# Softmax statistics of the plain attention heads: grouped scaling of maxima, a sum step for each tile, another order of the first head's tiles

## The chip, the cores and the metric

One core of a Trainium2 chip runs the whole program. The metric is device time in microseconds (us), the median of three runs. The engines named below are TensorE (PE, its weight loads PEld), VectorE (DVE), ScalarE (ACT), GpSimd (POOL) and SyncE (SP, which issues most DMAs).

## The reference, cut to what matters

Three stages follow one another. The first is attention over 4 batches of 8 heads, 576 rows of 64 columns each, with a mask in blocks of 64 rows. Only this stage is touched:

```python
scores = scale * np.matmul(q, k.transpose(0, 1, 3, 2))
scores = np.where(mask, scores, -1000000000.0)
scores = scores - np.max(scores, axis=-1, keepdims=True)
attn = np.exp(scores)
attn = attn / (np.sum(attn, axis=-1, keepdims=True) + 1e-09)
return np.matmul(attn, v)
```

The second stage is `h = max(x@w1, x@w2, x@w3)` and `h @ w_out` over all 2304 rows (512 to 768 to 512). The third sends each row to its two best of 8 experts (512 to 1024 to 512) and adds the weighted results.

## The kernel before, in words

**Attention.** A head has 576 rows, which is four and a half tiles of 128 rows. Tiles 0 and 1 see at most 256 keys; tiles 2, 3 and 4 see up to 384, 512 and 576 keys. The heads of the first batch (`i < NF`, NF = 8) are "plain": their scores are one float32 matmul. From the second batch on, heads use a split into two float32r parts and, for tiles 2 and 3, a fused VectorE instruction for the maximum.

- `s2(i)` (tile 4, 576 keys, in the two-bank PSUM tile `a2`), `s1(i)` (tile 2, 384 keys, one bank `s`) and `s3(i)` (tile 3, 512 keys, one bank `s`) make the scores and probabilities of the three large tiles of head i. Each calls `exps`: a maximum by VectorE (L240), its scaling by 0.125 (L241), and the exponential by ScalarE (L242), which also gives the sum of the row. Probabilities go to `Pa` and `Pb`, two of each.
- The three sums of a head lie in one statistics tile `st`. Only `s3` closes them: `inverse` adds 1e-9 (L245) and takes the reciprocal (L246) of three columns at once, and `scale_by` multiplies the three tiles (L253 on VectorE; L251 on ScalarE for tile 3 of the first three heads, `NRM[1]`).
- Tiles 0 and 1 are done two heads at a time: a "pair" gives four parts (128, 256, 128 and 256 keys) in `first_scores` (scores L444), which calls `soft`. The four pairs of the first batch come first in the program; their sums are not applied to the probabilities but spread by transposes (L522) in `first_rest`. The four pairs of the second batch are done beside plain heads 1 to 4, with scaling on VectorE. Pairs 1 and 3 of the first batch use the two banks of `a2`, the others two banks `s`.
- `t1` and `t2` transpose the probabilities (L304), `pv` multiplies them by the values (L357 for plain heads).

**Beside it.** `widen` converts the weights of the second stage: for each piece VectorE does L575 and L576, ScalarE L577 and L587, GpSimd L582, L585 and mostly L588. `hidden` (L662 to L664) is the second stage's first matmul; it needs a group of converted weights and finished rows of attention, and fills TensorE between the steps of the heads.

**What sets the order.** The loop over heads runs the steps of the string `ORDER = 's2 s1 g fr g t1 s3 t2 g fv fs g p g v pf g'`; s2, s1 and s3 there are those of head i+1, `g` is a piece of weight conversion and of the second stage, `fs` and `fr` are the pairs. Ahead of the loop, head 0 gets s2, s1, s3 by hand. This program order is only a priority: a planner goes through it with planned durations, and on every engine puts forward later work when earlier work is not ready by its plan. The order in which it leaves the instructions is then fixed for each engine, and each engine carries them out strictly in that order. Statistics tiles `st` have three buffers, so a fourth must wait until the first is released.

Of the kernel before, what the change touches and what calls it, by code (L numbers as in the profile page):

```python
# [13 lines left out]
AF = mybir.ActivationFunctionType  # L14
OP = mybir.AluOpType
AX = mybir.AxisListType
# [20 lines left out]
NF = 8  # L37
# [4 lines left out]
NRM = (0, 3, 0, 0)  # L42
# [7 lines left out]
NP, NK, NQ = 2, 2, 2  # L50
# [5 lines left out]
def plain(ap):  # L56
    return ap.bitcast(F32)
# [3 lines left out]
def tile_attention_moe_moe(ctx, tc, qT, kT, v, w1, w2, w3, w_out, gates, noise, e1, e2, out):  # L61
    nc = tc.nc
# [80 lines left out]
    PA = [att.tile([128, 384], F32, name=f"Pa{j}") for j in range(NP)]  # L143
    PB = [att.tile([128, 1088], F32, name=f"Pb{j}") for j in range(NP)]
# [44 lines left out]
    def prep_head(i):  # L189
        if i < NF:  # L190
            QK[i] = RAW.pop(i)
            return
        q, k = RAW.pop(i)
        Qs = att.tile([128, 384], F32R, name="Qs", bufs=NQ)
        Kh = att.tile([128, S], F32R, name="Kh", bufs=NK)
        Kl = att.tile([128, S], F32R, name="Kl", bufs=NK)
        nc.scalar.activation(Qs, q, AF.Copy)
        nc.scalar.activation(Kh, k, AF.Copy)
        nc.gpsimd.tensor_sub(Qs[64:], q[64:], plain(Qs[64:]))
        nc.gpsimd.tensor_sub(Kl, k, plain(Kh))  # L200
        QK[i] = (Qs, Kh, Kl)
# [9 lines left out]
    def masked(ps, o):  # L211

        nc.tensor.matmul(ps[:, o:o + 64], mL, mask[:, 448:], start=False, stop=True)

    def scores(ps, i, t, k0, k1, diag=None):
        if i < NF:
            q, k = QK[i]
            nc.tensor.matmul(ps, q[:D, 128 * t - 256:128 * t - 128], k[:D, k0:k1], start=True, stop=diag is None)
            if diag is not None:
                masked(ps, diag)  # L220
            return
        Qs, Kh, Kl = QK[i]
        lt = Qs[:, 128 * t - 256:128 * t - 128]
        nc.tensor.matmul(ps, lt, Kh[:, k0:k1], start=True, stop=False)
        nc.tensor.matmul(ps, lt, Kl[:, k0:k1], start=False, stop=True)

    def stats():
        return att.tile([128, 4, 4], F32, name="st", bufs=3)

    def exps(st, j, src, dst, fused):  # L230
        scale = 0.125
        if fused:

            w = src.shape[-1]
            nc.vector.tensor_tensor_reduce(out=dst, in0=src, in1=mask[:, 512 - w:], scale=-scale, scalar=3.0e38,
                                           op0=OP.add, op1=OP.min, accum_out=st[:, 1, j:j + 1])
            src, scale = dst, -1.0
        else:
            ax = AX.XY if len(src.shape) == 3 else AX.X
            nc.vector.tensor_reduce(st[:, 0, j:j + 1], src, axis=ax, op=OP.max, negate=True)  # L240
            nc.vector.tensor_scalar(st[:, 1, j:j + 1], st[:, 0, j:j + 1], scale, None, op0=OP.mult)  # L241
        nc.scalar.activation(dst, src, AF.Exp, bias=st[:, 1, j:j + 1], scale=scale, accum_out=st[:, 2, j:j + 1])  # L242

    def inverse(st, n):
        nc.vector.tensor_scalar(st[:, 2, :n], st[:, 2, :n], 1.0e-9, None, op0=OP.add)  # L245
        nc.vector.reciprocal(st[:, 3, :n], st[:, 2, :n])  # L246
        return st[:, 3]

    def scale_by(st, j, dst, norm=False):
        if norm:  # L250
            nc.scalar.activation(dst, dst, AF.Copy, scale=st[:, 3, j:j + 1])  # L251
        else:
            nc.vector.tensor_scalar(dst, dst, st[:, 3, j:j + 1], None, op0=OP.mult)  # L253

    def soft(parts, scaled=True, fused=False):
        st = stats()
        for j, (src, dst) in enumerate(parts):
            exps(st, j, src, dst, fused)
        inv = inverse(st, len(parts))
        if not scaled:  # L260

            return inv
        for j, (src, dst) in enumerate(parts):
            scale_by(st, j, dst)

    def bank(kind="m"):
        n, c = TAGS[kind]
        return (psS if n == "s" else psT).tile([128, 512], F32, name=n, bufs=c)


    ST = {}

    def s1(i):
        ps = bank("s")[:, :384]
        scores(ps, i, 2, 0, 384, 320)
        exps(ST[i], 1, ps, PA[i % NP], i >= NF)

    def s3(i):
        Pa, Pb, st = PA[i % NP], PB[i % NP], ST.pop(i)
        ps = bank("s")  # L280
        scores(ps, i, 3, 0, 512, 448)
        exps(st, 2, ps, Pb[:, 576:], i >= NF)

        inverse(st, 3)
        scale_by(st, 0, Pb[:, :576])
        scale_by(st, 1, Pa)
        scale_by(st, 2, Pb[:, 576:], i < NRM[1])

    def s2(i):
        Pb = PB[i % NP]  # L290
        ST[i] = stats()
        ps = psS.tile([128, 2, 512], F32, name="a2")
        scores(ps[:, 0, 0:288], i, 4, 0, 288)
        scores(ps[:, 1, 0:288], i, 4, 288, 576)
        exps(ST[i], 0, ps[:, :, 0:288], Pb[:, :576].rearrange("p (a b) -> p a b", a=2), False)

    POFF = {2: (PA, 0), 3: (PB, 576), 4: (PB, 0)}

# [133 lines left out]
    def first_scores(data, P, two=False, scaled=True):  # L432
        q, k = data[:2]
        parts = []
        if two:
            pair = psS.tile([128, 2, 512], F32, name="a2")
        for r in range(2):
            m = slice(64 * r, 64 * r + 64)
            ps = pair[:, r] if two else bank("s")
            for t in range(2):  # L440
                o = 128 * t
                n = o + 128
                a, b = (q, k[:, r]) if len(k.shape) == 3 else (q[m], k[m])
                nc.tensor.matmul(ps[:, o:o + n], a[:, o:o + 128], b[:, :n], start=True, stop=False)  # L444
                masked(ps, o + n - 64)
                parts.append((ps[:, o:o + n], P[:, 384 * r + o:384 * r + o + n]))
        return soft(parts, scaled)


    FR, FQ, FT = {}, {}, []  # L450
# [33 lines left out]
    def f_scores(b, h):  # L484
        Qs, Kh, Kl, _ = FQ[b, h]
        ps = bank("s")
        for t in range(2):
            p, lt = ps[:, 256 * t:256 * t + 256], Qs[:, 128 * t:128 * t + 128]
            nc.tensor.matmul(p, lt, Kh, start=True, stop=False)
            nc.tensor.matmul(p, lt, Kl, start=False, stop=True)  # L490
        soft([(ps[:, 0:128], FP[:, 0:128]), (ps[:, 256:512], FP[:, 128:384])], fused=True)
# [374 lines left out]
    def weights(n):  # L866
        for _ in range(n):
            next(conversion, None)

    weights(1)  # L870
    warm(bank(), WM[0])
    inv = first_scores(FIRST[0], PB[0], A2 & 1, False)
    for j in range(4):
        weights(WS[0])
        if j < 3:
            nxt = first_scores(FIRST[j + 1], PB[(j + 1) % NP], A2 >> (j + 1) & 1, False)
        first_rest(FIRST[j], PB[j % NP], PB[j % NP], 0, j, inv)
        inv = nxt
        weights(WS[1])
# [3 lines left out]
    load_head(1)  # L883
    load_values(1)
    weights(WS[4])
    s2(0)
    s1(0)
    s3(0)
    prep_head(1)
    weights(WS[2])  # L890
    cost = [0.0]
# [21 lines left out]
    for i in range(NH):  # L913
        b, h = divmod(i, H)
# [16 lines left out]
        for o in ORDER.split():  # L931
# [11 lines left out]
            elif o == "pf":  # L943
                if i + 1 in FI:
                    prep_f(*FI[i + 1])
                if i + 2 in FI:
                    load_f(*FI[i + 2])
            elif o == "fs":
                if i in AI:
                    first_scores(later.pop(), FP)  # L950
                    if order:
                        later.append(load_later(*order.pop(0)))
                if i in FI:
                    f_scores(*FI[i])
            elif o == "fr":
                if i - 1 in AI:
                    fb, j = AI[i - 1]
                    first_rest(now.pop(), FP, FP, 2 * fb, j)
                    if j == 3:
                        ready.add(2 * fb)  # L960
                if i in AI:
                    now.append([load_later_v(*AI[i])])
                if i - 1 in FI:
                    f_turn(*FI[i - 1])
            elif o == "fv":
                if i - 1 in FI:
                    f_values(*FI[i - 1])
            elif o[0] == "t":
                (t1, t2)[int(o[1]) - 1](i)
            elif i + 1 < NH:  # L970
                {"s1": s1, "s2": s2, "s3": s3}[o](i + 1)
# [16 lines left out]
    def bank2():  # L988
        turn[0] ^= 1
        if turn[0]:  # L990
            return ps2.tile([128, 512], F32, name="b")
        return psT.tile([128, 512], F32, name="t", bufs=4)
# [150 lines left out]
    ps = bank2()  # L1143
# [77 lines left out]
    with tc.If(full > 0):  # L1221
# [10 lines left out]
        with tc.For_i(0, E) as e:  # L1232
# [4 lines left out]
            with tc.For_i(0, NT) as t:  # L1237
# [6 lines left out]
                ps = ps3.tile([128, 4, 128], F32, name="pa")  # L1244
# [66 lines left out]
```

## Time and profile before

| | us |
|---|---|
| median of 3 runs | 1087.37 |
| lowest and highest | 1085.68, 1087.65 |
| the profiled execution | 1087.95 |
| its span | 1086.1 |
| PE busy in the span | 1034.8 |
| DVE, ACT, POOL busy | 537.9, 459.1, 533.3 |

The profiled execution's time has 1.85 us around its span. The plain heads and the pairs lie in the first 215 us; after that come the heads of the other batches (up to 543 us) and the experts.

### The profile page before, as it was taken

The page shows a single profiled execution, that of the slowest core. Times are in us where ns is not written, and L with a number is a line of the kernel's source. Part 1 is how long each engine was busy: PE and PEld are TensorE (multiplying, and loading weights), DVE is VectorE, ACT ScalarE, POOL GpSimd, SP SyncE. Part 2 cuts the span into 40 slices and gives each one's busy share as a digit, 9 for nine tenths or more (in the row PEclk, how much of TensorE's full clock was granted, in tenths as well). Part 3 has the DMA queues.
Part 4 walks back from the last instruction along what each step waited for, and adds up shares of the span by engine and source line. Part 5 has one row for each costly group of instructions (what it writes and reads, how often), then busy time and mean ns, then how long its engine had stood idle before and what let it go on. Part 6 is the DMA issues. An engine that isn't in the chain of part 4 may idle for free. (4 is left out here: it accounts for less than half of the span.)

```text
span 1086.1 us, 18720 instructions
## 1 busy us (share of the span) xinstructions
PE 1034.8 (95%) x6721; PEld 917.4 (84%) x6721; DVE 537.9 (50%) x1552; ACT 459.1 (42%) x1138; POOL 533.3 (49%) x465
## 2 busy tenths in 40 slices
PE   8799999999979999799999999989999999999997
PEld 4466678998879989799999997979898898989895
DVE  7789746596796887756333632222132222222221
ACT  5656555565765666554311433323232322323110
POOL 4447503455556464451321448877474646656302
PEclk7698999998989999899999999999999999999999
DMA  9533312152442323211020236655443444443101
GB/s 232 160 93 125 106 47 63 34 157 58 144 150 65 113 63 100 70 26 39 24 80 21 69 118 206 198 167 169 130 159 121 143 146 146 137 136 114 57 20 63
DMA packets 78513, 115.93 MB, mean 107 GB/s; under 512 B 17976, under 2 KB 48184, under 8 KB 78416
## 3 DMA queue, kind: packets, MB, share of 16 engines
q1 hardware_dynamic: 67824, 85.28, 26.3%
q0 software_dynamic: 10592, 29.41, 8.3%
q8 instruction: 54, 0.88, 0.3%
q14 instruction: 43, 0.35, 0.1%
HBM read 95.18 MB, written 20.53 MB: 107 GB/s over the span
## 5 line engine op out<-in xcount | busy, mean ns | idle before, releaser
L132 POOL TENSOR_TENSOR w<-rw,w 128x1536 fp32r<-128x1536 f32 (+1 forms) x45 | 141.1, 3142 | 74.2 <-ACT w L131 63.9
L131 ACT ACTIVATE w<-rw 128x1536 fp32r<-128x1536 f32 (+1 forms) x45 | 60.2, 1343 | 114.4 <-DMA rw<-in_e 65.0
L662 PE MATMUL t<-xA,w 128*128 128x256 f32 x360 | 105.2, 294 | 1.5 <-ACT w L587 0.8
L664 PE MATMUL t<-xA,w 128*128 128x256 f32 x360 | 103.9, 289 | 0.0
L663 PE MATMUL t<-xA,w 128*128 128x256 f32 x360 | 103.7, 289 | 0.1
L1041 PE MATMUL b<-xh,w 128*128 128x384 f32 (+7 forms) x272 | 86.8, 320 | 0.9 <-ACT xh L1031 0.9
L1042 PE MATMUL b<-xl,w 128*128 128x384 f32 (+7 forms) x272 | 86.9, 320 | 0.2 <-DVE xl L1032 0.2
L1043 PE MATMUL b<-xh,w 128*128 128x384 f32 (+7 forms) x272 | 86.9, 319 | 0.0
L662 PE MATMUL t<-xB,w 128*128 128x256 f32 x288 | 83.7, 291 | 1.4 <-DVE st L241 1.2
L677 POOL TENSOR_TENSOR hl<-hm,hh 128x512 fp32r<-128x512 f32 x24 | 31.6, 1318 | 105.2 <-ACT hh L676 105.2
L663 PE MATMUL t<-xB,w 128*128 128x256 f32 x288 | 82.7, 287 | 0.0
L664 PE MATMUL t<-xB,w 128*128 128x256 f32 x288 | 82.3, 286 | 0.0
L1090 POOL DMA_INDIRECT out_rows<-y,isc x40 | 40.5, 1013 | 79.9 <-DVE y L1089 72.6
L1046 DVE SCALAR_TENSOR_TENSOR ht<-b,ht 128x384 fp32r<-128x384 f32 (+6 forms) x56 | 29.1, 519 | 97.5 <-ACT ht L1045 97.5
L669 DVE TENSOR_TENSOR hm<-t,hm 128x512 f32<-128x512 f32 x54 | 37.2, 690 | 72.1 <-PE t L664 64.1
L662 PEld LDWEIGHTS t<-xA,w 128*128 128x128 f32 x360 | 69.6, 194 | 3.7 <-ACT w L587 0.9
L1085 PE MATMUL b<-w,ht 128*128 128x512 f32 (+1 forms) x168 | 67.1, 400 | 3.6 <-ACT ht L1045 3.6
L664 PEld LDWEIGHTS t<-xA,w 128*128 128x128 f32 x360 | 69.9, 194 | 0.5 <-issue 0.4
L663 PEld LDWEIGHTS t<-xA,w 128*128 128x128 f32 x360 | 69.9, 194 | 0.4 <-POOL xA L516 0.3
L1089 DVE SCALAR_TENSOR_TENSOR y<-b,idt,prev 128x512 f32<-128x512 f32 (+1 forms) x24 | 18.0, 750 | 104.8 <-PE b L1087 83.9
L1043 PE MATMUL t<-xh,w 128*128 128x256 f32 x240 | 67.4, 281 | 0.0
L1042 PE MATMUL t<-xl,w 128*128 128x256 f32 x240 | 67.4, 281 | 0.0
(383 smaller groups left out, 3245.8 us busy)
## 6 DMA issues: line engine op xcount, KB each, us to landing
rw<-in_e SPq DMA_DIRECT2D x32, 768.0 KB
xB<-in_w SPq DMA_DIRECT2D x36, 256.0 KB
rw<-in_e SPq DMA_DIRECT2D x16, 512.0 KB
rk<-in_kT SPq DMA_DIRECT2D x48, 144.0 KB
rq<-in_qT SPq DMA_DIRECT2D x48, 96.0 KB
x2d<-x SPq DMA_DIRECT2D x18, 256.0 KB
out_rows<-x SPq DMA_DIRECT2D x9, 512.0 KB
rv<-in_v SPq DMA_DIRECT2D x24, 160.0 KB
```

What stands on the lines that cost most here:

```text
L131: nc.scalar.activation(t[:, 0, :c], r[:, :c], AF.Copy)
L132: nc.gpsimd.tensor_sub(t[:, 1, :c], r[:, :c], plain(t[:, 0, :c]))
L662: nc.tensor.matmul(ps[:, j], wh, x[:, 0], start=kt == 0, stop=False)
L663: nc.tensor.matmul(ps[:, j], wh, x[:, 1], start=False, stop=False)
L664: nc.tensor.matmul(ps[:, j], wl, x[:, 0], start=False, stop=kt == 3)
L669: nc.vector.tensor_max(m, ps, m)
L677: (nc.vector if u == NU - 1 else nc.gpsimd).tensor_sub(l, m, plain(a))
L1041: nc.tensor.matmul(p, wt1(e, 0, kt, f), th[:, kt, c0:c1], start=kt == 0, stop=False)
L1042: nc.tensor.matmul(p, wt1(e, 0, kt, f), tl[:, kt, c0:c1], start=False, stop=False)
L1043: nc.tensor.matmul(p, wt1(e, 1, kt, f), th[:, kt, c0:c1], start=False, stop=kt == 3)
L1085: nc.tensor.matmul(ps, a, wt2(e, 0, f), start=f == 0, stop=False)
L1090: st = nc.gpsimd.indirect_dma_start(out=out, out_offset=bass.IndirectOffsetOnAxis(ap=isc[:n, e, c:c + 1], axis=0), in_=y, in_offset=None, ...
```

## The change: what it does

`soft`, which serves the pairs, now finds all maxima of its group first, scales them in one instruction of as many columns as there are parts, and then does the exponentials. The plain heads no longer go through `exps` and the joint `inverse`: each of s1, s3 and s2 calls `soft` with one part, so each tile has its own statistics tile, its own 1e-9 step, its own reciprocal and its own scaling. Which of them ScalarE scales stays as it was (tile 3 of heads 0 to 2). From the second batch on the joint sums remain. In front of the loop, head 0's tiles come in the order s1, s3, s2.

```diff
-    def soft(parts, scaled=True, fused=False):
-        st = stats()
-        for j, (src, dst) in enumerate(parts):
-            exps(st, j, src, dst, fused)
-        inv = inverse(st, len(parts))
+    def soft(parts, norm=False, scaled=True, fused=False):
+        st, n = stats(), len(parts)
+        if fused:
+            for j, (src, dst) in enumerate(parts):
+                exps(st, j, src, dst, True)
+        else:
+            for j, (src, dst) in enumerate(parts):
+                ax = AX.XY if len(src.shape) == 3 else AX.X
+                nc.vector.tensor_reduce(st[:, 0, j:j + 1], src, axis=ax, op=OP.max, negate=True)
+            nc.vector.tensor_scalar(st[:, 1, :n], st[:, 0, :n], 0.125, None, op0=OP.mult)
+            for j, (src, dst) in enumerate(parts):
+                nc.scalar.activation(dst, src, AF.Exp, bias=st[:, 1, j:j + 1], scale=0.125,
+                                     accum_out=st[:, 2, j:j + 1])
+        inv = inverse(st, n)
...
-            scale_by(st, j, dst)
+            scale_by(st, j, dst, norm)
...
     def s1(i):
...
-        exps(ST[i], 1, ps, PA[i % NP], i >= NF)
+        if i < NF:
+            soft([(ps, PA[i % NP])], i < NRM[0])
+        else:
+            exps(ST[i], 1, ps, PA[i % NP], True)
...
     def s3(i):
...
-        exps(st, 2, ps, Pb[:, 576:], i >= NF)
+        if i < NF:
+            soft([(ps, Pb[:, 576:])], i < NRM[1])
+            return
+        st = ST.pop(i)
+        exps(st, 2, ps, Pb[:, 576:], True)
...
     def s2(i):
...
-        exps(ST[i], 0, ps[:, :, 0:288], Pb[:, :576].rearrange("p (a b) -> p a b", a=2), False)
+        part = ps[:, :, 0:288], Pb[:, :576].rearrange("p (a b) -> p a b", a=2)
+        if i < NF:
+            soft([part], i < NRM[2])
+        else:
+            ST[i] = stats()
+            exps(ST[i], 0, *part, False)
...
-        return soft(parts, scaled)
+        return soft(parts, False, scaled)
...
-    s2(0)
     s1(0)
     s3(0)
+    s2(0)
```

## Rows read from the trace of the kernel before

**Rows 1.** The page: busy us of each engine (share of the span) and instructions.
```profile
PE 1034.8 (95%) x6721; PEld 917.4 (84%) x6721; DVE 537.9 (50%) x1552; ACT 459.1 (42%) x1138; POOL 533.3 (49%) x465
```

**Rows 2.** Stretches: length, busy us of PE, PEld, DVE, ACT, POOL (instructions), granted clock, DMA.
```profile
0.00:54.00 54.00, 42.15 (x152) 25.67 (x153) 39.46 (x123) 33.41 (x98) 24.64 (x35) 0.72 0.73 197
20.00:25.00 5.00, 4.01 (x12) 2.25 (x13) 4.71 (x15) 5.00 (x19) 4.02 (x5) 0.67 0.94 187
70.00:130.00 60.00, 56.03 (x295) 37.96 (x294) 56.56 (x118) 34.68 (x94) 42.52 (x45) 0.91 0.42 128
130.00:215.00 85.00, 84.95 (x571) 68.47 (x570) 43.69 (x160) 42.19 (x125) 21.69 (x21) 1.00 0.17 48
```

**Rows 3.** Waits of PE, first 54 us: who for whom, total us, times, longest.
```profile
PE a L218 <- ACT Pb L242: 2.5, 1, 2.5
PE s L218 <- ACT Pb L242: 0.8, 1, 0.8
```

**Rows 4.** Groups of DVE by form, 0 to 215 us: busy us, mean ns, idle before.
```profile
L241 DVE TENSOR_SCALAR st<-st 128x1 f32<-128x1 f32 x58 | 8.1, 145 | 0.6
L245 DVE TENSOR_SCALAR st<-st 128x4 f32<-128x4 f32 x8 | 3.2, 400 | 0.8 <-ACT fP L242 0.7
L245 DVE TENSOR_SCALAR st<-st 128x3 f32<-128x3 f32 x10 | 2.1, 207 | 5.6 <-ACT Pb L242 5.6
L246 DVE RECIPROCAL st<-st 128x3 f32<-128x3 f32 x9 | 1.6, 173 | 0.2
```

**Rows 5.** Timeline, pair 0: start us, length us, instruction, idle before it.
```profile
11.08 0.29 DVE L575 TENSOR_SCALAR hm<-xB 128x256 int32<-128x256 int32 x1 [2.52 <-DMA xB<-in_w]
11.35 0.41 DVE L240 TENSOR_REDUCE st<-s 128x1 f32<-128x256 f32 x1
11.47 0.47 ACT L242 ACTIVATE Pb<-s,st 128x256 f32<-128x256 f32 x1
12.09 0.80 PE L444 MATMUL s<-w 128*128 128x128 f32 x2 [2.03 <-ACT Pb L242]
```

**Rows 6.** Timeline of ACT: three exponentials back to back.
```profile
20.75 0.36 ACT L242 ACTIVATE Pb<-a,st 128x128 f32<-128x128 f32 x1
21.09 0.48 ACT L242 ACTIVATE Pb<-s,st 128x256 f32<-128x256 f32 x1
21.54 0.38 ACT L242 ACTIVATE Pb<-s,st 128x128 f32<-128x128 f32 x1
```

**Rows 7.** Timeline: a four-column step of DVE and POOL beside it.
```profile
24.98 1.45 POOL L588 TENSOR_TENSOR w<-x,w 128x512 fp32r<-128x512 f32 x1 [0.30 <-DVE xB L576]
25.22 1.24 DVE L245 TENSOR_SCALAR st<-st 128x4 f32<-128x4 f32 x1
```

**Rows 8.** Timeline, pair 3 and what follows on PE.
```profile
44.91 0.41 DVE L240 TENSOR_REDUCE st<-a 128x1 f32<-128x256 f32 x1
...
45.54 0.47 ACT L242 ACTIVATE Pb<-a,st 128x256 f32<-128x256 f32 x1
...
46.16 2.28 PE L218 MATMUL a<-Kl,Qs 64*128 64x288 f32 x4 [2.48 <-ACT Pb L242]
...
50.34 0.56 PE L662 MATMUL t<-xA,w 128*128 128x256 f32 x1
```

**Rows 9.** Timeline, head 0: scores of tile 3, first scaling, first transposes.
```profile
28.88 1.12 PE L218 MATMUL s<-Kl,Qs 64*128 64x512 f32 x2
...
51.53 0.52 DVE L253 TENSOR_SCALAR Pb<-Pb,st 128x576 f32<-128x576 f32 x1
...
56.47 0.38 PE L304 MATMUL t<-ident,Pb 128*128 128x128 f32 x2
```

**Rows 10.** Timeline of DVE, 74 to 130 us: first and last of four sum steps.
```profile
85.24 0.57 DVE L245 TENSOR_SCALAR st<-st 128x4 f32<-128x4 f32 x1
...
124.60 0.17 DVE L245 TENSOR_SCALAR st<-st 128x3 f32<-128x3 f32 x1 [0.45 <-ACT Pb L242]
```

**Rows 11.** Waits of PE, 54 to 130 us.
```profile
PE s L218 <- ACT fP L242: 0.6, 1, 0.6
```

More of the change, by code (lines that the diff above doesn't have):

```diff
@@ L275, in s1 @@
         scores(ps, i, 2, 0, 384, 320)
-        exps(ST[i], 1, ps, PA[i % NP], i >= NF)
+        if i < NF:
+            soft([(ps, PA[i % NP])], i < NRM[0])
+        else:
+            exps(ST[i], 1, ps, PA[i % NP], True)
     def s3(i):
-        Pa, Pb, st = PA[i % NP], PB[i % NP], ST.pop(i)
+        Pa, Pb = PA[i % NP], PB[i % NP]
         ps = bank("s")
         scores(ps, i, 3, 0, 512, 448)
-        exps(st, 2, ps, Pb[:, 576:], i >= NF)
+        if i < NF:
[3 more added lines that the diff above has]
+        exps(st, 2, ps, Pb[:, 576:], True)
         inverse(st, 3)
@@ L286, in s3 @@
         scale_by(st, 1, Pa)
-        scale_by(st, 2, Pb[:, 576:], i < NRM[1])
+        scale_by(st, 2, Pb[:, 576:])
     def s2(i):
         Pb = PB[i % NP]
-        ST[i] = stats()
         ps = psS.tile([128, 2, 512], F32, name="a2")
```

## The prediction

> **What bounds the kernel now.** I read the page's busy shares first: TensorE is busy for 1034.8 of 1086.1 us, so about 51 us of idle time is all that lies outside it; VectorE, which the change edits, is busy for half the span [rows 1]. Shares over the span say nothing about a change that ends at 215 us, so the view of stretches came next. From 130 to 215 us TensorE is busy for 84.95 of 85 us at a granted clock of 1.00 while VectorE has half its time free: what VectorE does there a little earlier or later is hidden. From 70 to 130 us VectorE is nearly full (56.56 of 60 us), mostly with the conversion of weights. The first 54 us are the loose part: TensorE is busy for 42.15 us only, at a granted clock of 0.72, and VectorE is full in parts of it (4.71 of 5 us from 20 to 25) [rows 2]. So the change is paid or repaid before 130 us, and what counts there is when TensorE is let go. The view of waits names two things in the first 54 us that this change touches: TensorE waits 2.5 us and 0.8 us for exponentials to leave a PSUM bank [rows 3]; a third such wait, 2.03 us, stands in the timeline at 12.09 [rows 5].
>
> **The change part by part.** All durations are of the profiled execution (1087.95 us, span 1086.1).
>
> *Fewer scalings in the pairs.* A one-column scaling takes 0.145 us, four of them 0.58 us. The grouped step is a four-column TENSOR_SCALAR on the same tile; the row nearest to it is the 1e-9 step of the pairs, mean 0.400 us [rows 4]. That saves 0.18 us for each of 8 pairs. Its bounds are far apart: an unhindered four-column step of 0.16 us would save 0.42, one like that at 25.22 (1.24 us) would cost 0.66 [rows 7]. The mean of eight is the nearest row, so I take 0.18. The four front pairs save 0.7 us, and as VectorE is full for about half of that time I count **-0.4 us** (for the four pairs, bounds -1.7 and +2.6).
>
> The 1.24 us step began at 25.22 and ended when the GpSimd subtraction that ran from 24.98 to 26.43 had ended, while the 58 one-column steps average 0.145 us [rows 4, 7]. The Trainium skill, "SBUF — State Buffer", section "Who interferes with whom", says that a tensor_scalar in a two-port mode and a GpSimd instruction exclude one another for the whole instruction. The trace agrees with it, and the rule speaks against this part of the change: it trades steps that never blocked for one that can. By it, with every front step held as at 25.22, the part would be +2.6 us instead of -0.4; if none met a GpSimd instruction it would be -1.7.
>
> *The first exponentials of a pair wait for its last maximum.* Before, each part goes to ScalarE as soon as its own maximum is scaled. The four maxima of a pair are not close together on VectorE, because weight steps stand between them.
> - Pair 3: its last maximum begins at 44.91 and takes 0.41 us; its last exponential runs from 45.54 to 46.01 and lets TensorE into `a2` at 46.16 for tile 4 of head 0 [rows 8]. Afterwards all four exponentials come behind that maximum and a step of 0.40 us, so from 45.72 on. Back to back, a part of 128 keys takes 0.34 us and one of 256 keys 0.45 us from start to start (20.75, 21.09, 21.54) [rows 6]: 0.34 + 0.45 + 0.34 + 0.47 = 1.60, so they end at 47.32 instead of 46.01, 1.3 us later. Behind that matmul stand on TensorE the rest of pair 3 and, at 50.34, the first matmul of the second stage. Lower bound 0, if later work makes it good; I take the whole: **+1.3 us**.
> - Pair 0: before, VectorE stood 2.52 us at L575 for a DMA of weights, with the pair's last maximum behind it (11.35 to 11.76), and the exponential at 11.47 released TensorE at 12.09 [rows 5]. With the group, the two exponentials of that bank begin after 11.76 plus about 0.24 and end 0.34 + 0.47 later, at 12.8 instead of 11.94: +0.9 us. If the planner sets all maxima and their scaling ahead of the blocked L575, the exponentials are over by 11 us and the 2.0 us wait goes. Between -2.0 and +0.9 I take **+0.4 us**: the order of before has the DMA step in front of the fourth maximum, and there is still other idle time to take up half.
> - Pairs 1 and 2: one wait of 0.8 us for an exponential [rows 3]; lengthened by a third or so, **+0.3 us**, between -0.8 and +1.0.
> - The four later pairs: one wait of 0.6 us of TensorE for the exponentials of `fP` [rows 11]; a bunch instead of a row makes it longer, **+0.4 us** (between -0.6 and +1.3, the price found for pair 3); what lies behind 130 us costs nothing, as TensorE has other work.
>
> *A sum step for each tile.* Before, a plain head has one three-column 1e-9 step (0.207 us) and one reciprocal (0.173): 0.38 us. Afterwards three one-column steps; by L241, the one-column form of the same operation, 0.145 us, and by the reciprocal of three columns 0.173 (a one-column reciprocal has no row; if it took the 0.145 us of the one-column step, a head would be 0.08 us cheaper): 3 x 0.318 = 0.95 us [rows 4]. So +0.57 us a head, 8 x 0.57 = 4.6 us in all, against 8 x 0.18 saved. It counts where VectorE is full: from 70 to 130 us there are four sum steps, of two heads and two pairs [rows 10], so 2 x 0.57 - 2 x 0.18 = **+0.8 us**. Behind these steps on VectorE stand L575 and L576, and those who wait for them are GpSimd's L582 to L588 and then the second stage's matmuls. Bounds 0 (TensorE has enough else) and +4.6.
>
> *New waits.* Each 1e-9 step waits for its own exponential's sum. Before, the ten three-column steps waited 5.6 us of VectorE's time [rows 4]. Now two more for each head may wait, with the next tile's maximum or a weight step behind them. Where VectorE has room it costs nothing; I count 0 and keep a rival for it.
>
> *The tiles are scaled earlier.* The number of scalings is the same. For head 0 the first scaling runs at 51.53 and the first transpose of it at 56.47 [rows 9]: nobody waits for a scaling, so an earlier one gains 0. If the 4.9 us between them went, the joint scaling would be late, and this part a gain.
>
> *Third tile in front, tile 4 last.* In the trace the scores of tile 3 of head 0 already run at 28.88 and those of tile 4 at 46.16 [rows 8, 9], although the program has tile 4 first: it waits for `a2`. **0 us.** No DMA is moved.
>
> **The sum:** -0.4 + 1.3 + 0.4 + 0.3 + 0.4 + 0.8 = +2.8 us on 1087.95, 1090.75. The profiled execution is 0.58 us above the median of the runs, so the forecast for the median is 1090.2 us.
>
> **The rivals.**
> - *Hidden.* The front runs 1 to 2 us late, but the idle time of TensorE before 54 us (54 - 42.15 = 11.9 us) and its choice of other work take it up. For it: most of that idle time is other waits. Against it: the first matmul of the second stage stands behind tile 4 of head 0 in a fixed order [rows 8]. The time is 1087.4.
> - *Faster.* The planner puts the grouped scaling of pair 0 ahead of the weight step that waits for its DMA. The wait of 2.03 us goes [rows 5], with it the 0.4 us of VectorE time and half of the 0.8 us wait of the pairs in between [rows 3]; the other parts stay hidden: -2.8 us on 1087.4, 1084.6. For it: three scalings fewer stand in front of the fourth maximum. Against it: the weight steps are earlier in the program and so have priority.
> - *Clearly slower.* Three statistics buffers serve four groups of a head and its pair instead of two. A maximum then cannot start until the tile three groups back is scaled, its bank stays taken, and TensorE stops at the next scores. The price is the wait of a sum step for its exponential, 5.6 us over ten steps or 0.56 us each [rows 4]: two more for a head make 1.12 us, for the five heads ahead of 130 us 5.6 us, on top of the sum above: 1095.8. It decides as soon as the fourth group is planned before the first is scaled. Against it: in a plain head each group is closed at once, so that buffers come free sooner than before.
> - That the change does nothing is part of the first rival: for the order of head 0's tiles I expect just that.
>
> **How the numbers follow.** A measurement of this kernel can tell about 0.2% (2.2 us) from no change: below 1085.2 is faster, above 1089.5 slower. The forecast gets 0.38 (0.36 of it slower, 0.02 same; its own range 1088.6 to 1093), hidden 0.24 (0.20 same, 0.02 on each side), faster 0.22, clearly slower 0.16. That makes faster 0.24, same 0.22, slower 0.54. The order of every engine is planned anew, so waits beyond the plain heads can move too; the range goes from 1083.5, which holds the faster case, to 1097, which holds the clearly slower one, and leaves out less than 2 in 10.
>
> **What would show it.** The four exponentials of pair 3 in a row behind its last maximum, tile 4 of head 0 at about 47.4 instead of 46.16, and the first L662 near 51.6; the grouped step at 0.16 to 1.2 us; DVE busier by about 3 us (4.6 - 1.4) before 215 us. I am wrong if L662 starts no later than at 50.3, if pair 0's exponentials all end before 11.5, or if the difference arises behind 215 us.

## The result: faster, where slower was forecast

The changed kernel takes 1076.98 us (median of 5 executions, 1073.34 to 1078.80) against 1087.65 us for the kernel before beside it; the ratio is 0.9892, 95% interval 0.9867 to 0.9918. A second round of it gave 1077.00 us, 0.9917 (0.9898 to 0.9935). The forecast was 1090.2 us, and 1077 lies below the whole range.

### The profile page after: what moved, and what is told of

Its sections match the earlier page's. It is cut to its first block, busy times and chain, and to the rows that moved or that the text cites. A ratio compares the mean times of both kernels' runs of the same rounds, so it can differ in the third digit from the quotient of the medians.

```text
span 1075.3 us, 18730 instructions
## 1 busy us (share of the span) xinstructions
PE 1025.3 (95%) x6721; PEld 910.7 (85%) x6721; DVE 530.2 (49%) x1560; ACT 457.3 (43%) x1138; POOL 532.2 (49%) x465
## 5 line engine op out<-in xcount | busy, mean ns | idle before, releaser
L682 PE MATMUL t<-xA,w 128*128 128x256 f32 x360 | 104.9, 292 | 0.1
L682 PE MATMUL t<-xB,w 128*128 128x256 f32 x288 | 83.3, 289 | 1.4 <-DVE st L241 1.2
L683 PEld LDWEIGHTS t<-xA,w 128*128 128x128 f32 x360 | 69.1, 192 | 1.9 <-DVE xA L573 1.1
L682 PEld LDWEIGHTS t<-xA,w 128*128 128x128 f32 x360 | 68.8, 192 | 1.9 <-issue 0.8
L684 PEld LDWEIGHTS t<-xA,w 128*128 128x128 f32 x360 | 68.7, 191 | 0.4 <-POOL w L608 0.3
```

What stands on the lines that cost most here:

```text
L682: nc.tensor.matmul(ps[:, j], wh, x[:, 0], start=kt == 0, stop=False)
L683: nc.tensor.matmul(ps[:, j], wh, x[:, 1], start=False, stop=False)
L684: nc.tensor.matmul(ps[:, j], wl, x[:, 0], start=False, stop=kt == 3)
```

## The profile after

The page's busy times [rows 1], and the stretches that answer to [rows 2]:

```profile
PE 1025.3 (95%) x6721; PEld 910.7 (85%) x6721; DVE 530.2 (49%) x1560; ACT 457.3 (43%) x1138; POOL 532.2 (49%) x465
```
```profile
0.00:54.00 54.00, 41.85 (x198) 25.16 (x198) 41.62 (x134) 36.03 (x109) 25.81 (x35) 0.94 0.73 202
20.00:25.00 5.00, 3.01 (x16) 1.75 (x16) 4.90 (x13) 4.20 (x13) 3.90 (x5) 1.00 0.81 153
70.00:130.00 60.00, 55.99 (x314) 39.83 (x315) 44.43 (x117) 35.32 (x103) 36.05 (x39) 0.91 0.36 109
130.00:215.00 85.00, 84.79 (x571) 70.36 (x572) 49.49 (x174) 43.33 (x127) 25.75 (x26) 0.98 0.20 56
```

TensorE is busy for as long as before in the first 54 us (41.85 and 42.15 us), but has done 198 matmul instructions instead of 152, at a granted clock of 0.94 instead of 0.72. From 70 to 130 us VectorE has 44.43 us of work instead of 56.56: that stage's work has moved forward.

To see where the gain arises I cut the span at two landmarks that every variant has: the first product of the second stage (L662 before, L682 after) and the first score of head 8. The two stretches between the cuts, before and then after (columns as in rows 2):

```profile
0.00:50.34 50.34, 38.49 (x139) 23.07 (x139) 38.06 (x118) 31.11 (x93) 24.64 (x35) 0.72 0.77 209
50.34:182.80 132.46, 127.89 (x735) 91.66 (x733) 94.79 (x256) 70.79 (x200) 52.73 (x55) 0.95 0.29 87
```
```profile
0.00:42.04 42.04, 30.68 (x142) 17.85 (x142) 30.30 (x102) 25.74 (x81) 19.45 (x29) 0.92 0.81 220
42.04:174.40 132.36, 126.95 (x729) 91.22 (x729) 94.39 (x281) 74.07 (x212) 57.56 (x61) 0.95 0.32 97
```

The second stretch is equal to 0.1 us (132.46 and 132.36). The first is 8.3 us shorter, with about as many matmuls in it (139 and 142). So 8.3 of the 10.8 us of the two spans (1086.1 and 1075.3) are won ahead of the first product of the second stage. The other 2.4 us lie behind head 8, where the two profiled runs of the changed kernel differ by more than that themselves (900.9 and 896.2 us from there to the end; 903.3 before), so no cause is sought for them.

What is late in the first stretch is seen in pair 3. The first line is its scores; its four maxima (DVE) and exponentials (ACT) stand in the timeline of the kernel before like this:

```profile
23.66 0.80 PE L444 MATMUL a<-w 128*128 128x128 f32 x2
...
30.05 0.28 DVE L240 TENSOR_REDUCE st<-a 128x1 f32<-128x128 f32 x1
35.14 0.35 ACT L242 ACTIVATE Pb<-a,st 128x128 f32<-128x128 f32 x1
37.66 0.41 DVE L240 TENSOR_REDUCE st<-a 128x1 f32<-128x256 f32 x1
39.53 0.47 ACT L242 ACTIVATE Pb<-a,st 128x256 f32<-128x256 f32 x1
41.45 0.28 DVE L240 TENSOR_REDUCE st<-a 128x1 f32<-128x128 f32 x1
42.66 0.35 ACT L242 ACTIVATE Pb<-a,st 128x128 f32<-128x128 f32 x1
```

and, with the last two in [rows 8], end at 46.01. Maximum and exponential alternate strictly, and the engine changes seven times. No step takes over 0.47 us; the time lies between the steps, where VectorE and ScalarE carry out, or wait with, other work that stands ahead in their orders. Most of it is conversion: from 30.05 to 45.6 us VectorE has 8.2 us of it (L575, L576, L588) and ScalarE 7.2 us (L577, L587). The alternation is no accident of one plan: in all ten kernels of the table below whose front pairs are not grouped, the maxima and exponentials of the pairs in `a2` alternate in this way. In pair 2, whose halves lie in two tiles `s`, the maximum of the second half (16.89) does precede the first exponential (18.75). Within one tile no maximum starts before the exponential of the part in front of it has ended, and where VectorE is early the wait for it shows (last line, a later pair):

```profile
16.89 0.28 DVE L240 TENSOR_REDUCE st<-s 128x1 f32<-128x128 f32 x1
...
18.75 0.36 ACT L242 ACTIVATE Pb<-s,st 128x128 f32<-128x128 f32 x1
...
112.52 0.42 DVE L240 TENSOR_REDUCE st<-s 128x1 f32<-128x256 f32 x1 [0.60 <-ACT fP L242]
```

The Trainium skill, "PSUM — Partial Sum Buffer", section "PSUM bank collisions raise a hardware error", says that no two of the three engines may be in one bank on the same partitions at the same time, two readers included, and that the compiler's scheduler therefore puts an order between them. The trace agrees for the parts of a bank (112.52); that the parts of the two banks of `a2` alternate too (39.53, then 41.45) goes beyond the page.

After the change:

```profile
17.30 0.49 PE L464 MATMUL a<-w 128*128 128x128 f32 x2 [0.20 <-ACT Pb L266]
...
23.36 1.14 DVE L263 TENSOR_REDUCE st<-a 128x1 f32<-128x128 f32 x4
24.80 0.58 DVE L264 TENSOR_SCALAR st<-st 128x4 f32<-128x4 f32 x1
25.48 0.37 ACT L266 ACTIVATE Pb<-a,st 128x128 f32<-128x128 f32 x1 [0.46 <-PE t L542]
25.84 0.47 ACT L266 ACTIVATE Pb<-a,st 128x256 f32<-128x256 f32 x1
33.64 0.37 ACT L266 ACTIVATE Pb<-a,st 128x128 f32<-128x128 f32 x1 [0.51 <-PE t L565]
34.07 0.47 ACT L266 ACTIVATE Pb<-a,st 128x256 f32<-128x256 f32 x1
36.78 1.23 PE L218 MATMUL a<-Kl,Qs 64*128 64x288 f32 x4
42.04 0.38 PE L682 MATMUL t<-xA,w 128*128 128x256 f32 x1
```

The four maxima come in a row (x4, 1.14 us), one scaling follows, and the engine changes once. From the first maximum to the end of the last exponential it is 11.2 us instead of 16.0, and since pair 1 has left `a2` earlier in the same way, the scores of pair 3 run 6.4 us earlier (17.30 instead of 23.66) and its maxima begin 6.7 us earlier. The exponentials are still in two groups, 7 us apart, with other work of ScalarE between them. Tile 4 of head 0 starts at 36.78 instead of 46.16, the first product at 42.04 instead of 50.34.

The waits of TensorE in the first 54 us (answering to rows 3) and the small steps on VectorE up to 215 us (to rows 4):

```profile
PE t L542 <- DVE st L246: 3.5, 3, 1.3
PE s L464 <- ACT Pb L266: 2.1, 1, 2.1
...
PE s L218 <- ACT Pb L266: 1.1, 2, 0.7
```
```profile
L246 DVE RECIPROCAL st<-st 128x1 f32<-128x1 f32 x24 | 3.8, 157 | 0.4
L245 DVE TENSOR_SCALAR st<-st 128x1 f32<-128x1 f32 x24 | 3.5, 147 | 3.0 <-ACT Pa L266 2.2 <-ACT Pb L266 0.7
L264 DVE TENSOR_SCALAR st<-st 128x1 f32<-128x1 f32 x24 | 3.4, 145 | 0.1
L264 DVE TENSOR_SCALAR st<-st 128x4 f32<-128x4 f32 x8 | 2.8, 353 | 0.1
```

The wait of tile 4 for `a2` (2.5 us) is gone; the waits of L542 for the reciprocals of the pairs (3.5 us) are new in this run.

## The experiments

The theories named in the expectations: A, the row of maxima lets the pairs end earlier; B, the granted clock of the first 54 us is the cause; C, the sums of each tile; D, a hole in the weight conversion on VectorE (in the kernel before its 20th piece, L575, starts at 64.19 only) sets the end; E, less VectorE work in the later pairs; F, behind the hole TensorE sets the pace. H came last: from the first product of the second stage to head 8 it is a fixed time plus what TensorE loses by a lower clock.

All runs in one table, with medians and ratios to the kernel before on the same chip. "First product" and "to head 8" are the cuts of above in the profiled run, "clock loss" is the length of the second stretch times (1 minus its granted clock, a figure of two digits, so good to some 0.7 us), "last piece" the start of the last conversion step.

| kernel | median us | ratio, 95% interval | first product | to head 8 | clock loss | last piece |
|---|---|---|---|---|---|---|
| before | 1087.37 | 1 | 50.3 | 132.5 | 6.6 | 123.4 |
| changed | 1076.98 | 0.9892 (0.9867 to 0.9918) | 42.0 | 132.4 | 6.6 | 112.4 |
| after_again | 1077.00 | 0.9917 (0.9898 to 0.9935) | 42.9 | 130.4 | 5.2 | 113.0 |
| g_only | 1079.85 | 0.9940 (0.9916 to 0.9963) | 40.7 | 134.7 | 6.7 | 114.8 |
| g_front | 1078.14 | 0.9920 (0.9900 to 0.9939) | 41.2 | 133.9 | 8.0 | 115.8 |
| gs_only | 1074.99 | 0.9883 (0.9864 to 0.9901) | 44.6 | 127.5 | 1.3 | 113.1 |
| gs_full | 1082.25 | 0.9961 (0.9944 to 0.9978) | 43.5 | 132.6 | 6.6 | 115.2 |
| gs_fill_gate | 1082.25 | 0.9960 (0.9936 to 0.9984) | 45.2 | 135.2 | 5.4 | 114.5 |
| after_earlier | 1084.35 | 0.9979 (0.9957 to 1.0001) | 44.1 | 137.4 | 9.6 | 111.7 |
| after_fill_gate | 1076.69 | 0.9913 (0.9892 to 0.9934) | 45.5 | 129.5 | 1.3 | 115.7 |
| t_only | 1080.04 | 0.9945 (0.9926 to 0.9964) | 46.5 | 129.6 | 2.6 | 115.3 |
| t_head0 | 1085.78 | 0.9990 (0.9972 to 1.0009) | 49.3 | 134.5 | 8.1 | 119.8 |
| t_later | 1088.33 | 1.0008 (0.9986 to 1.0029) | 49.1 | 134.6 | 6.7 | 123.0 |
| o_only | 1086.23 | 0.9992 (0.9973 to 1.0012) | 51.4 | 132.4 | 6.6 | 122.9 |
| g_later | 1087.35 | 0.9997 (0.9976 to 1.0018) | 48.3 | 133.9 | 8.0 | 120.6 |
| before_a2 | 1085.43 | 0.9993 (0.9975 to 1.0012) | 45.7 | 133.0 | 8.0 | 118.2 |
| before_earlier | 1087.34 | 1.0001 (0.9979 to 1.0024) | 53.4 | 130.1 | 2.6 | 116.8 |
| before_fill_gate | 1085.61 | 0.9985 (0.9967 to 1.0003) | 50.9 | 130.6 | 2.6 | 122.2 |
| before_dummies | 1087.57 | 1.0001 (0.9985 to 1.0017) | 51.4 | 134.2 | 10.7 | 126.2 |

Executions of one kernel lie up to 10 us apart (before: 1083 to 1093), so a single profiled run is read for where things start, and the median for the time.

The table falls into two groups. In the nine rows with grouped front pairs (the changed kernel twice, `g_only`, `g_front`, `gs_only`, `gs_full`, `gs_fill_gate`, `after_earlier`, `after_fill_gate`) the first product starts between 40.7 and 45.5, and all ratios lie between 0.9883 and 0.9979. In the ten others it starts between 45.7 and 53.4, and the ratios lie between 0.9985 and 1.0008, but for `t_only` (0.9945). Tile 4 of head 0 starts between 34.7 and 38.6 in the first group and between 42.5 and 49.4 in the second, `before_a2` (23.0) aside. So the earlier front is no luck of a single plan; how much of it is left at the end differs from plan to plan.

**Each part alone.** The kernel before with the row of maxima (`g_only`), with the sums of each tile (`t_only`), with the new order of head 0 (`o_only`); these are the hunks of the diff shown in front, one at a time.

> Of the change only the grouping is made: in soft, all maxima of a pair, then one scaling, then the exponentials. Plain heads keep their joint sums, head 0 keeps its order. Theory A (the grouping gives every engine another order in the front, in which the pairs are done earlier): 5 to 11 us faster than before, first matmul of the second stage near 42 to 44 us instead of 50.3. Theory B (the gain is the granted clock of the first 54 us, 0.94 instead of 0.72, whatever the order): the time follows that clock; with 0.72 it stays at 1087. Theory C (the sums by tile are what gains): within 2 us of before. The forecast on record: about 2 us slower.

> Of the change only the sum step for each tile of the plain heads is made; pairs keep a scaling for each maximum, head 0 keeps its order. Theory A: within 2 us of before. Theory C: 5 to 11 us faster. The forecast on record: 0.8 us slower.

> Of the change only the order of head 0 is made (tile 4 last); grouping and sums stay as before. All theories: within 1 us of before, as the scores of tile 4 run last already.

Grouping alone gives 0.9940, sums alone 0.9945, the order nothing. Their sum, 1.15%, is about what the whole change gives (1.08 and 0.83%), so A and C both seem to hold. The later runs do not bear that sum out.

**Which pairs.** `g_front` groups only in the pairs of the first batch (`scaled` is false there), `g_later` only in the second batch's.

```diff
-        if fused:
+        if fused or scaled:          # g_front
+        if fused or not scaled:      # g_later
...
-                exps(st, j, src, dst, True)
+                exps(st, j, src, dst, fused)
```

> Grouping only, and only for the four pairs of the first batch; all else as before. Theory D (what decides is the hole in the conversion of weights on VectorE, from 38.9 to 64.2 us before and from 41.9 to 53.6 us after: VectorE's fixed order puts the 20th piece behind maxima of later heads, which wait for TensorE; from there the rest takes about 59 us in every run, and the end moves with it; grouping the front pairs lets their scores run earlier and shortens the hole): hole ends near 55, 6 to 9 us faster than before. Rival E (the gain is less VectorE work in the full stretch, in which the later pairs lie): within 2 us of before.

> Grouping only, and only for the four pairs of the second batch. Theory D: hole ends near 64 as before, time within 2 us of before. Rival E: 4 to 8 us faster.

The four front pairs hold all of it (0.9920, not told apart from the whole change), the later ones nothing (0.9997).

**Order or number of instructions.** `gs_only` has the maxima in a row, but scales each by itself, so that no instruction is saved.

```diff
-            nc.vector.tensor_scalar(st[:, 1, :n], st[:, 0, :n], 0.125, None, op0=OP.mult)
+            for j in range(n):
+                nc.vector.tensor_scalar(st[:, 1, j:j + 1], st[:, 0, j:j + 1], 0.125, None, op0=OP.mult)
```

> Before, with the maxima of a pair in a row and the exponentials behind them, but a one-column scaling for each part: no instruction fewer than before. Theory A (the order counts: maxima of one bank no longer wait for the exponential in front of them): pair 3's scores start ahead of 20 us instead of 23.66, tile 4 of head 0 near 36 instead of 46.2, conversion goes on at about 55 to 57 instead of 64.19, and the time is 1078 to 1081.5. Rival (three scalings fewer make VectorE's room): as before, 1085 to 1089.

1074.99 us, 3 us below the range that Theory A expected: the order is what counts. The maxima in a row and tile 4 of head 0:

```profile
23.77 1.14 DVE L263 TENSOR_REDUCE st<-a 128x1 f32<-128x128 f32 x4
...
35.92 1.24 PE L218 MATMUL a<-Kl,Qs 64*128 64x288 f32 x4
```

The rival, that three scalings fewer make the room, is out. Next to `g_only` (1079.85), from which it differs by the scalings alone, it is even 4.9 us faster.

**The bank of pair 3, and the clock.** `before_a2` (`A2 = 2`) puts pair 3 into two banks `s`, so that tile 4 of head 0 need not wait for it; `before_dummies` (`WM = (14, 0, 8, 0, 0)`) adds 64 products of ones in front of the transposes of the front pairs, which changes no value.

> The kernel before with one size changed: pair 3 of the first batch uses two banks s instead of the two banks of a2 (A2 = 2 instead of 10), so that tile 4 of head 0 needs not wait for pair 3's exponentials. Theory D: tile 4's scores of head 0 run ahead of 40 us instead of at 46.2, the load of head 2 and the maxima of the next heads come earlier, the hole ends 5 to 10 us earlier and the time falls by as much. Rival E: no change beyond 2 us.

> The kernel before, with 8 more matmuls of ones (128x512, result not used) ahead of each half of a pair's transposes in the first batch: 64 in all, to keep TensorE busy while it waits for the softmax. Theory B (clock): granted clock of the first 54 us above 0.9, and 4 to 9 us faster than before although 64 x 0.22 = 14 us of matmuls were added. Theory A (order): not faster; with 12 us of idle time to lie in, 0 to 8 us slower.

In `before_a2` tile 4 starts at 23.0 instead of 46.2, yet the median is not told apart from before (the profiled run, 1080.97, is the fastest of its ten). The last exponential of pair 3 ends there at 42.2, against 46.0 before and 34.5 after the change: an early tile 4 while pair 3 stays late is worth little. The stretches of `before_dummies`:

```profile
0.00:51.40 51.40, 43.18 (x205) 23.75 (x206) 35.45 (x118) 32.41 (x97) 24.46 (x35) 0.97 0.74 208
51.40:185.60 134.20, 130.15 (x732) 92.49 (x731) 94.47 (x256) 69.12 (x195) 52.50 (x55) 0.92 0.29 85
```

The clock of the first stretch is 0.97 instead of 0.72, and the first product is no earlier (51.4 and 50.3). The added products took part of the gained time themselves; but tile 4 of head 0, which waits for VectorE and ScalarE alone, starts at 43.7, 2.5 us earlier, where the change brings 9.4. The second profiled run of the changed kernel (after_again) tells the same without added work:

```profile
0.00:42.88 42.88, 34.95 (x142) 21.11 (x142) 31.66 (x105) 27.02 (x84) 19.93 (x29) 0.80 0.78 215
```

Its clock is 0.80 up to the first product where the first run had 0.92, and that product starts at 42.88 instead of 42.04. Theory B falls for the front.

**The conversion.** `before_lean_pieces` leaves out L576 from the 20th piece on; its weights are then other numbers and the whole takes 4900 us, because experts' loops run longer, so only its front is read. `before_earlier` and `after_earlier` ask for four more pieces ahead of the loop over heads.

```diff
+        PIECE.append(0)                       # before_lean_pieces
+        if len(PIECE) <= 19:
             nc.vector.scalar_tensor_tensor(hi, hi, -0x40000000, t, op0=OP.bitwise_and, op1=OP.bitwise_or)
...
-WS = (2, 0, 4, 2, 4)
+WS = (2, 0, 8, 2, 4)                          # before_earlier, after_earlier
```

> The kernel before, in which the pieces of weights from the 20th on leave out one of their two steps on VectorE (L576, 29 x 0.66 = 19 us; these weights are then not the right ones). Theory D, second half (behind the hole the conversion paces the end): the hole stays at about 64, the last piece is begun 10 to 19 us earlier than at 123.4, and the time falls by 4 to 15 us. Rival F (behind the hole TensorE's own work paces): the last piece is begun earlier but the time stays within 2 us.

> Before, with four more pieces of weight conversion asked for ahead of the loop over heads (8 instead of 4); the pairs and the plain heads stay as they were, and VectorE's order then has 23 pieces ahead of the hole instead of 19. Theory D (the number of pieces behind the hole, at some 2.1 us each on VectorE, sets the end): four pieces fewer, the last one 5 to 8 us earlier than 123.42 although the hole stays as long, and 1079 to 1083. Rival 1 (the hole is a symptom; the late heads set the end): 1086 to 1089. Rival 2 (the added pieces make VectorE fuller ahead of the hole and push pair 3 and the hole back by as much): the hole ends at 70 or later, 1085 to 1089.

> The changed kernel, with four more pieces asked for ahead of the loop. Theory D: the last piece comes 5 to 8 us earlier than 112.43 and the time is 1069 to 1073. Theory F (with the hole as short as this, TensorE and not the conversion paces): the last piece is earlier, the last product of the split heads is not, and the time stays at 1075 to 1079.

Until then the span had ended 960.3 to 963.2 us after the last piece in all nine kernels, and I held Theory D for proved. `before_lean_pieces` seemed to agree (last piece 16.3 us earlier, head 8 7.9). `before_earlier` speaks against it. VectorE's pieces there, around the hole:

```profile
44.97 1.97 DVE L575 TENSOR_SCALAR hm<-xB 128x256 int32<-128x256 int32 x2
67.07 0.28 DVE L575 TENSOR_SCALAR hm<-xB 128x256 int32<-128x256 int32 x1
```

The hole is there and ends 2.9 us later, four pieces more lie ahead of it, the last piece comes 6.6 us earlier, and the time is the same to 0.01%. In `after_earlier` the last piece is 0.8 us earlier than in the changed kernel, and the time 7 us longer. So the last piece does not set the end. That both went together because both follow the front fits the table, where in `before_earlier` the first product comes 3.1 us later, but is not shown by a run of its own.

**The sum that fits.** In the table the time to head 8 minus the clock loss is 125.0 to 128.2 us for 17 of the 19 rows, whatever the edit; the others are `gs_fill_gate` (129.8, with 16 products of ones in it), `before_dummies` (123.5) and, not in the table, `before_lean_pieces` (123.0, with work left out). TensorE is idle for only 3.7 to 7.8 us of that stretch in these rows, so it is at work for nearly all of it. The next runs test the clock as a cause: eight products of ones (128x512, overwritten) where TensorE stands idle at the gates' first product and the clock falls, in the kernel before, in `gs_only` (with eight more in front of the 128x128 transposes), and in the changed kernel.

```diff
             ps = bank()
+            warm(ps, 8 if g == 0 else 0)
             for k in range(2):
                 nc.tensor.transpose(ps[:, 2 * E * k:2 * E * k + 2 * E], p[:, 128 * k:128 * k + 128],
```

> Before, with eight products of ones by ones (128x512, overwritten afterwards) on TensorE in front of the 16x16 transposes L640 of the gates' first part, where it is idle for 1.78 and 0.81 us and where the granted clock then lies between 0.66 and 0.85 from 75 to 100 us (5.2 us lost in the profiled run). Theory H (head 8 starts some 126 us after the first L662, plus what the clock loses behind 50 us): the clock stays near 1.00 from 80 us on, the mean clock of the executions rises from 0.969 to 0.972 or more, and the time is 1082 to 1085.5. Rival (the clock only goes along; VectorE and its conversion set the pace there): clock up, idle time up by as much, 1086.5 to 1089.5.

> The kernel with the maxima of a pair in a row and one-column scalings, with the same eight products of ones and eight more in front of the 128x128 transposes of the gates' first part, before which TensorE is idle for 3.29 us. Theory H: the clock there lost 1.7 us at most, so 1072.5 to 1075. Rival: as without them or later by their own length, 1075 to 1078.

> The changed kernel with eight products of ones by ones (128x512, overwritten) behind the first gate product, in the 3.64 us in which TensorE waits for the exponentials of a pair; behind that wait the clock was 0.76, 0.50 and 0.72 in three stretches of 5 us (5.1 us lost in the profiled run). Theory H: less clock lost from 70 to 90 us, mean clock above that of after_again, and a time 2 to 4 us below after_again, 1072 to 1075. Rival (the clock only goes along): as after_again within 1 us, or later by up to the 3 us of the products.

> The changed kernel itself once more, as the neighbour of after_fill_gate on the same chip: 1074 to 1079, with a mean clock of 0.973 to 0.978 against 0.969 for the kernel before, and a span without the clock's loss some 3.4 us below that of before.

The stretch around the gate, for the kernel before and for `before_fill_gate`, then for after_again and `after_fill_gate`:

```profile
75.00:100.00 25.00, 22.33 (x96) 14.33 (x94) 24.28 (x56) 12.45 (x36) 16.95 (x18) 0.80 0.43 130
```
```profile
75.00:100.00 25.00, 22.94 (x111) 13.12 (x110) 23.39 (x57) 13.63 (x40) 17.46 (x19) 0.93 0.44 132
```
```profile
70.00:85.00 15.00, 11.53 (x47) 8.13 (x48) 12.74 (x39) 9.46 (x30) 9.17 (x11) 0.66 0.46 132
```
```profile
70.00:85.00 15.00, 12.57 (x63) 8.05 (x63) 14.77 (x37) 8.70 (x29) 10.74 (x13) 0.89 0.47 143
```

The clock rises as meant, from 0.80 to 0.93 and from 0.66 to 0.89, and the time to head 8 falls by 1.8 and 0.9 us though the eight products take some 2 us themselves (seven of them 2.22 us in `before_fill_gate` and 1.69 us in `after_fill_gate`). But the medians give 1.8 us for the kernel before, an interval that touches no change, and 0.3 us for the changed one, whose first product came later (45.5 against 42.9). That is what the rival had expected there, a clock that only goes along. `gs_fill_gate` lost 7 us against `gs_only`, outside both of its ranges. So the sum holds as an accounting of these runs, and that a higher clock there is worth its full loss is not shown.

**The sums of each tile.** `t_head0` and `t_later` have them in head 0 and in heads 1 to 7 alone; `gs_full` is the changed kernel whole, with one scaling for each maximum.

```diff
-        exps(ST[i], 1, ps, PA[i % NP], i >= NF)
+        if i in (0,):                         # t_head0; (1, ..., 7) in t_later; s2 and s3 alike
+            soft([(ps, PA[i % NP])], i < NRM[0])
+        else:
+            exps(ST[i], 1, ps, PA[i % NP], i >= NF)
```

> Before, with a statistics tile, a sum step and a reciprocal for each tile of head 0 alone; heads 1 to 7 keep the joint ones. If the gain of the tile sums comes from the front (tile 4 of head 0 no longer bound to its head's other tiles, and so a shorter hole): tile 4 near 42.5 instead of 46.2, the hole ends near 59, and the time is 1080 to 1083. If it comes from the later heads: hole and time as before, 1085 to 1089.

> Before, with a statistics tile, a sum step and a reciprocal for each tile of heads 1 to 7; head 0 keeps the joint ones. If the tile sums gain in these heads: 1079 to 1083, and by Theory H with the first L662 at 48 to 51 and no clock lost behind 90 us. If it takes all heads: 1085 to 1089.

> The changed kernel whole (tile sums and order of head 0 too), with a one-column scaling for each maximum instead of the one of several columns. If the tile sums add to the gain of the order of the maxima: 1069 to 1072.5. If, as Theory H has it, both work by the same first L662 and the same clock: 1073 to 1078.5, like the changed kernel and like gs_only.

Neither half gains (0.9990, 1.0008), though both together gave 0.9945; and with the sums the time is 1082.25 where `gs_only` has 1074.99, outside both ranges expected. Next to the changed kernel, `gs_full` differs by the scalings alone and is 5.3 us slower, while `gs_only` was 4.9 us faster than `g_only` by the same edit. So the sign of both small parts, the sums and the scalings, depends on the plan that they fall into. In `t_only` the first product comes 3.8 us earlier and the second stretch loses 4.0 us less by the clock; why its plan does that and those of its halves do not, stays open.

No version is faster than the changed kernel by more than the intervals can tell: `gs_only` has 0.9883 (0.9864 to 0.9901), the changed kernel 0.9892 (0.9867 to 0.9918) and 0.9917 (0.9898 to 0.9935).

## Why the prediction was wrong, point by point

- *"The first exponentials of a pair wait for its last maximum", pair 3, +1.3 us.* This step failed. It left the last maximum at 44.91 and asked what comes after it. But that maximum was itself the seventh link of a chain: it comes behind the exponential of the part before it, that one behind its own maximum, and so on back to 30.05. I had quoted the end of the chain [rows 8] and not its first six links. Measured, tile 4 of head 0 starts 9.4 us earlier instead of 1.2 later, the first L662 8.3 us earlier instead of 1.3 later; `g_front` and `gs_only` show that this is the change's gain. The four exponentials are not in a row either, as the prediction had them: two come from 25.48 on, two from 33.64 on.
- *Pair 0, +0.4 us; pairs 1 and 2, +0.3 us.* Right: TensorE waits for pair 0's bank until 12.64 instead of 12.09, and the waits of L218 for exponentials are 1.1 instead of 0.8 us. They are paid, and more than made good by pair 3, whose scores run 6.4 us earlier.
- *Fewer scalings, -0.4 us.* The four-column step takes 0.353 us on average (0.400 taken from rows 4), one beside GpSimd 1.26 us. The sizes were about right. What the part is worth in the time is not shown: without the saving `gs_only` is 4.9 us faster than `g_only`, and `gs_full` 5.3 us slower than the changed kernel.
- *Later pairs, +0.4 us.* `g_later` shows no cost, with an interval of some 2 us either way.
- *A sum step for each tile, +0.8 us.* The durations were right (0.147 and 0.157 us; 24 of each, 7.3 us, instead of 8 x 0.38 = 3.0), yet VectorE's busy time up to 215 us did not rise by 3 us: it is 150.51 after and 150.86 before, and up to the first score of head 8 it even falls, from 132.85 to 124.70 us. Steps that the change does not touch became shorter: the 48 first conversion steps (L575 before, L595 after) take 0.505 instead of 0.565 us on average, the 48 second ones (L576, L596) 0.612 instead of 0.657, together 5.2 us. `t_only` is faster by 6 us; the forecast had the wrong sign there, and the runs do not say why.
- *New waits, 0.* The 24 one-column steps wait for 3.0 us in all, with the three joint ones of later heads 4.7, less than the ten of before (5.6). The rival of three statistics buffers did not occur: the maxima of the changed kernel wait for TensorE's scores alone.
- *Order of head 0's tiles, 0.* Right: 0.9992 (0.9973 to 1.0012).
- *What I said would make me wrong:* "if L662 starts no later than at 50.3". It starts at 42.04. The rival "faster" had the sign, but another place and a quarter of the size: pair 0 and its DMA play no part.

## What to carry to other kernels

Where two engines take turns on the parts of one buffer, count the changes of engine and read the gaps between them before costing the steps: some 3 us of maxima and exponentials took 16 us here, since each change stood in a queue of other work. A step that looks late because of its predecessor should be followed back to the first of its kind. A quantity that moves one to one with the time in nine variants is still no cause until an edit moves it alone. And where a planner orders every engine anew after each edit, one variant proves little: compare groups of them, and landmarks in the span.

## What the runs showed of the hardware that was not expected

- The granted clock was 0.72 in the first 54 us of the kernel before, with three waits of TensorE of 2.0 to 2.6 us, and 0.94 and 0.84 in the two profiled runs of the changed kernel; over whole executions its mean was 0.969 (109 of before) and 0.975 (11 of the changed kernel). As lost time (span times one minus the clock) that is 33.7 and 27.4 us, 6.3 of the 11.1 us between the means. In the front the clock does not set when the first product starts (`before_dummies`, after_again).
- Around the gates' first product the clock falls again: in all 16 rows of the table without products of ones at the gate, the lowest 5 us between 65 and 100 us have a clock of 0.50 to 0.82. In the kernel before it falls ahead of an idle time (0.66 from 75 to 80 us, with TensorE busy, idle for 1.78 us before 81.88), in the changed kernel behind one (0.50 from 75 to 80 us, all of it at the lower of its two levels, after 3.64 us before 73.03). Filling that time brought the stretch from 0.80 to 0.93 and from 0.66 to 0.89.
